# Spectral filter with gated FFN: scratch laid out by sides, filters copied inside SBUF, the sine table turned by DMA

## The chip, the cores and the metric

The kernel runs on one core of one Trainium2 chip. The metric is device time in microseconds (us) of one execution; the figure of a kernel is the median of its runs. The profiled execution is one more run, with its own time, and every duration below comes from its trace. The engines are named as in the profile: PE (TensorE matmuls), PEld (its weight loads), DVE (VectorE), ACT (ScalarE), POOL (GpSimd) and SP (SyncE, which here only issues DMAs).

## The reference, cut to what matters

x is 2048 rows (S) of 640 (D). Each row is normalized; the result goes through a two-dimensional real FFT, a pointwise complex filter w_r + i w_i (2048 x 321) and the inverse FFT, and beside it through a gated feed-forward network with 1536 inner columns (F). The two meet in the last line.

```
xn = (x - mean) / sqrt(var + 1e-5)
s  = irfft2(rfft2(xn) * (w_r + 1j * w_i))
g  = silu((gelu(xn @ w_gate) * (xn @ w_up)) @ w_down)
out = x + s * g
```

## The kernel before

**The two streams of work.** The FFN is the bulk: four groups of four slabs (a slab is 128 rows of x, taken with a stride of 16: row 16*n2 + n1 belongs to slab n1). For each group, `ffn_half` makes 12 tiles of gate and up products (psg and psu, L714), ACT takes the GELU of the gate (L718), DVE multiplies (L720), and `down_third` multiplies with w_down (L738). These pieces, in order, form the list `back`, 144 steps. The spectral branch is written as small pieces between them: `put(s, f, ...)` in lines 795 to 899 places a piece behind step s, and the loop at the end of `build` (L911) runs the steps. The whole order on each engine is thus written by hand (manual schedule); every engine and SP works through its own list in that order, and waits where its next instruction's inputs are not there.

**The spectral branch.** The FFT along the rows (length 2048 = 128 x 16) is done in two stages, with a product along the columns (length 640) between them.
- `tinv_sin` makes the sine table Tinv (128 x 16 x 128, bf16) on ACT, and `tfwd` turns it: for each of two halves, eight TensorE transposes into PSUM (L326) and one DVE copy into Tfwd (L327). They stand behind steps 26 and 27, between pieces of the first group's w_down product.
- `slab_S1` (from step 30 on) multiplies one folded slab with its part of Tfwd (pz, L484); ACT copies the result to zbuf (L486).
- `group_D` takes one slab first and then three at a time through the column transform FT (`d_group`, L494 and L498), copies to the buffer zd, and stores to the DRAM scratch ZDR, one store for each slab (L512). zd and zbuf lie in GEN, a buffer whose place B2 takes later.
- `load_B2` (behind step 56) reads ZDR back in another order, so that the second stage finds its 16 x 2 x 2 x 2 index combinations on the partitions: ten loads into 64 partitions each (L530). The stored order has re/im outermost, and the side (bit 5 of the row index) inside.
- `s2_in` and `s2_out` do the second stage and the filter in 11 bursts: products px (L556), an ACT copy xs (L564), two DVE multiplications with W1 and W2 (L568), products pu (L583), ACT copies, and stores to the scratch UDR (L592), 64 partitions each.
- `load_V` (behind step 89) reads UDR into one tile V in B2's place, in five pieces of 2, 2, 4, 4 and 4 slabs, re and im apart: ten loads (L603). `gather` (DVE, L613) picks the columns that don't fill a chunk; `slab_S1i` (L631), `group_Di` and the rest invert the transform and finish the rows.

**The filters.** W1 and W2 (128 x 2 x 16 x 322, bf16, 321 columns used) hold w_r and w_i so that the partition's two low bits are ri (re or im) and pm (row u or its mirror image 128 − u). `w_rows` loads them straight from DRAM, in rows of 321 elements (642 bytes) into 16 partitions of one half (hh); since both values of ri want the same data, each row is read twice. There are 18 loads for each filter: W1's behind steps 8 to 15, W2's behind 32 to 47. `w_edge` (POOL, L127) then halves the first and last column.

**Queues.** All DMAs are issued from SP, in one order; each also waits for the DMA issued eight places before it (eight semaphores are used in turn). The DMA transposes of slabs (`slab_T` with eng 2, L465: one 128 x 640 slab into xnT, five 128 x 128 blocks) stand in the same queue. xnT1, for the second FFN group, is made by the four of steps 17 to 23 and is first read at step 36.

Of the kernel before, what the change touches and what calls it, by code (L numbers as in the profile page):

```python
# [14 lines left out]
P = 128  # L15
S = 2048
D = 640
L = 321
# [12 lines left out]
@with_exitstack  # L31
def kernel(
    ctx: ExitStack,
    tc: tile.TileContext,
    A_x: bass.AP,
    A_w_r: bass.AP,
    A_w_i: bass.AP,
    B_x: bass.AP,
    B_w_gate: bass.AP,
    B_w_up: bass.AP,  # L40
    B_w_down: bass.AP,
    out: bass.AP,
):
# [26 lines left out]
    W2 = wts.tile([P, 2, NS, LP], BF16)  # L70
    wgv = B_w_gate.rearrange("(c p) f -> p c f", p=P)
    wuv = B_w_up.rearrange("(c p) f -> p c f", p=P)
    with tc.manual_schedule():
        build(nc, locals())


def build(nc, env):
# [33 lines left out]

    def w_rows(i, hh, ri, pm):
        WT, sp = spw[i]
        p0 = hh * 64 + ri * 2 + pm
        for lo in range(2):
            u0 = lo * 32 + hh * 16
            if pm == 0:
                nc.sync.dma_start(out=WT[p0:p0 + 61:4, lo, :, 0:L], in_=sp[:, u0:u0 + 16, :])
            elif u0 == 0:
                nc.sync.dma_start(out=WT[p0:p0 + 61:4, lo, 1:NS, 0:L], in_=sp[:, 127:112:-1, :])  # L120
                nc.sync.dma_start(out=WT[p0:p0 + 61:4, lo, 0, 0:L], in_=sp[:, 64, :])
            else:
                nc.sync.dma_start(out=WT[p0:p0 + 61:4, lo, :, 0:L], in_=sp[:, 128 - u0:112 - u0:-1, :])

# [108 lines left out]
    def affine(name, src, a, b):  # L233
# [84 lines left out]

    def tinv_sin():
        nc.scalar.activation(out=Tinv, in_=vt, func=ACT.Sin, bias=negpi, scale=TWO_PI / 2048.0)  # L320

    def tfwd(h):
        sl = slice(8 * h, 8 * h + 8)
        pt = psB.tile([P, 8, P], BF16, tag="b")
        for k in range(8):
            nc.tensor.transpose(out=pt[:, k, :], in_=Tinv[:, 8 * h + k, :], identity=ident)  # L326
        nc.vector.tensor_copy(out=Tfwd[:, sl, :], in_=pt)  # L327

# [129 lines left out]
    def slab_T(n1, eng):  # L458
# [17 lines left out]
    zbuf = fv.rearrange("p g l -> p (g l)").bitcast(BF16)[:, 0:4 * D].rearrange("p (s c k) -> p s c k", s=4, c=5)  # L476
    zdbuf = vt.rearrange("p n k -> p (n k)").bitcast(BF16)[:, 0:12 * LP].rearrange(
        "p (s a c l) -> p s a c l", s=2, a=3, c=2)

# [24 lines left out]
    def group_D(i):  # L504
        n0, n = DF[i]
        pd = d_group([Zt.pop(n0 + a) for a in range(n)], FT, LH)
        zd = zdbuf[:, i % 2, 0:n]
        for b in range(2):
            ev = nc.vector.tensor_copy if i in (2, 5) and b == 1 else nc.scalar.copy
            ev(out=zd.rearrange("p a c (m b) -> p a c m b", b=2)[:, :, :, :, b], in_=pd[b])  # L510
        for a in range(n):
            nc.sync.dma_start(out=ZDR[:, n0 + a].rearrange("c p l -> p c l"), in_=zd[:, a, :, 0:L])  # L512

# [10 lines left out]
    def load_B2():  # L524
        B2 = big.tile([P, NH, L], BF16, tag="sB", name="B2")
        zv = ZDR.rearrange("c n (z a k h) l -> a (c n z) k h l", z=2, a=2, k=2)
# [43 lines left out]

    uv = UDR.rearrange("c n (z a k h) l -> a (c n z) k h l", z=2, a=2, k=2)

    def s2_out(b):
# [16 lines left out]
        if l0 + w == L:  # L590
            for lo in range(2):
# [4 lines left out]
    VP = ((0, 2), (2, 2), (4, 4), (8, 4), (12, 4))  # L596
    VO = (0, L + 1, LH, L + 1 + HD)

    def load_V():
        V = big.tile([P, NS, 2 * L], BF16, tag="sB", name="Vin")  # L600
        for n0, n in VP:
            for c in range(2):
                nc.sync.dma_start(out=V[:, n0:n0 + n, c * L:c * L + L],  # L603
                                  in_=UDR[c].rearrange("n p l -> p n l")[:, n0:n0 + n, :])
        st_c["V"] = V
        st_c["Y"] = big.tile([P, NS, D], BF16, tag="sX", name="Yall")

    def gather(i):
        n0, n = VP[i]
        V = st_c["V"][:, n0:n0 + n, :]  # L610
        vr = work.tile([P, 4, P], BF16, tag="p1", bufs=2, name="vr")[:, 0:n, :]
# [14 lines left out]
    def slab_S1i(n1):  # L626
        V = st_c["V"]
        pv = psB.tile([P, 5, P], FP32, tag="b")
        for c in range(5):
            lhsT = V[:, n1, VO[c]:VO[c] + P] if c < 4 else st_c[("r", n1)]  # L630
            nc.tensor.matmul(pv[:, c, :], lhsT=lhsT, rhs=Tinv[:, n1, :], start=True, stop=True)  # L631
# [191 lines left out]
    put(23, fold_a, 0)  # L823
    for it in ((silu_table,), (tinv_sin,), (ft_sin, 0)):
        put(23, *it)
# [3 lines left out]
    put(25, fold_a, 1)  # L829
    put(26, tfwd, 0)  # L830
    put(27, tfwd, 1)
    put(27, norm, 8)
# [31 lines left out]
    for k in range(4):  # L864
        put(32 + 3 * k, slab_T, 8 + k, 2)
        put(65 + 3 * k, slab_T, 12 + k, 2)
    for k in range(16):
        put(8 + k if k < 8 else (32, 35, 38, 41, 44, 44, 47, 47)[k - 8], w_rows, k // 8, k % 8 // 4, k % 2, k % 4 // 2)
    put(40, w_edge, 0)
# [76 lines left out]
```

## Time and profile before

| | us |
|---|---|
| median of three runs (203.82 to 204.15) | 203.82 |
| the profiled execution | 204.42 |
| its span | 202.6 |
| PE busy | 195.6 |
| DVE busy | 129.3 |
| ACT busy | 122.4 |
| PE, L326 (the 16 transposes of Tinv) | 2 x 0.45 |
| DVE, L327 (two copies of 128 x 1024) | 2 x 0.69 |
| DVE, L568 (22 filter products, 646 ns each on average) | 13.3 |

The span is the time from the first instruction to the last; the execution's own time is larger by what lies around it (1.8 us). The page's busy figures are unions over the span, so an engine that is busy for 97% has almost no idle time to give back. In lists of groups, "x22 | 13.3, 646" means 22 instructions, 13.3 us in all, 646 ns on average, followed by the idle time of the engine before them and what ended it. In a timeline a line begins with the start and the duration in us. SPq lines are issues of DMAs: their duration is the time that SP needed to issue them, not that of the transfer; the time to landing is given in the DMA view.

### The profile page before, as it was taken

The numbers are of one execution on the slowest core, as the hardware profiler recorded it, in microseconds if no ns is written. First come the engines' busy times: TensorE is split into PE (matmuls) and PEld (weight loads), VectorE is DVE, ScalarE is ACT, GpSimd is POOL, SyncE is SP. The second block draws the span as 40 slices with busy tenths as digits, with TensorE's granted clock in tenths as the row PEclk, the third lists the DMA queues.
The fourth block names the chain that finished last, engine by engine and source line by source line (L and its number), as shares of the span: only waits on it lengthen the run. The fifth ranks groups of instructions, "written<-read, shape, count | busy, mean of one in ns | idle before, by whom it ended". The sixth has DMA issues, their size and how long they took to land.

```text
span 202.6 us, 4209 instructions
## 1 busy us (share of the span) xinstructions
PE 195.6 (97%) x1574; PEld 119.8 (59%) x1589; DVE 129.3 (64%) x340; ACT 122.4 (60%) x208; POOL 33.4 (16%) x61
## 2 busy tenths in 40 slices
PE   7899999999999999999999999999999999999993
PEld 5688854777555555566644333457775555556762
DVE  7886966786488982533576465342358776867672
ACT  2448657857886768423788688425375647476631
POOL 5327779953000200100000000000000000000000
PEclk9999999999999999999999999999999999999999
DMA  5999999899799999729995233569501334224211
GB/s 167 306 297 305 372 310 142 158 147 137 153 170 143 173 174 174 180 43 226 213 228 111 44 97 101 130 164 317 172 0 68 97 102 127 69 92 144 86 69 60
DMA packets 43315, 31.77 MB, mean 157 GB/s; under 512 B 12192, under 2 KB 41504, under 8 KB 43296
## 3 DMA queue, kind: packets, MB, share of 16 engines
q1 hardware_dynamic: 43296, 31.52, 71.4%
q8 instruction: 12, 0.20, 0.4%
q14 instruction: 7, 0.06, 0.1%
HBM read 21.66 MB, written 7.88 MB: 146 GB/s over the span
## 4 chain that ended last, share of the span: by engine, by line
PE 90%; DVE 4%; DMA 2%; issue 1%; POOL 1%; SPq 0%; ACT 0%; DVEq 0%
PE psu L714 25%; PE psg L714 24%; PE psg L738 13%; PE psu L738 12%; PE pd L494 5%; PE pz L484 2%; PE pv L631 2%; PE pu L583 2%; DMA X<-in_A_x_dram 2%; PE px L556 2%; PE pd L498 2%; DVE st L174 1%; DVE uT L720 1%; POOL rst L190 1%; PE pt L326 0%
## 5 line engine op out<-in xcount | busy, mean ns | idle before, releaser
L714 PE MATMUL psu<-xnT,Wu 128*128 128x512 bf16 (+2 forms) x289 | 60.9, 339 | 0.6 <-issue 0.2
L714 PE MATMUL psg<-xnT,Wg 128*128 128x512 bf16 (+2 forms) x286 | 60.4, 338 | 0.9 <-issue 0.5
L720 DVE TENSOR_TENSOR uT<-psu,ge 128x512 bf16<-128x512 f32 (+2 forms) x59 | 34.3, 585 | 29.8 <-PE psu L714 22.5
L718 ACT ACTIVATE ge<-psg 128x512 bf16<-128x512 f32 (+2 forms) x59 | 30.5, 518 | 27.6 <-PE psg L714 25.9
L738 PEld LDWEIGHTS <-uT 128*128 128x128 bf16 x384 | 36.3, 98 | 14.6 <-issue 0.6
L714 PEld LDWEIGHTS <-Wu 128*128 128x128 bf16 x295 | 26.6, 98 | 22.9 <-issue 2.7
L714 PEld LDWEIGHTS <-Wg 128*128 128x128 bf16 x295 | 26.6, 98 | 21.9 <-issue 1.5
L738 PE MATMUL psg<-Wd,uT 128*128 128x320 bf16 (+1 forms) x192 | 30.3, 302 | 0.0
L738 PE MATMUL psu<-Wd,uT 128*128 128x320 bf16 (+1 forms) x192 | 29.2, 296 | 0.0
L568 DVE TENSOR_TENSOR X<-xs,W 128x972 bf16<-128x972 bf16 (+2 forms) x22 | 13.3, 646 | 10.6 <-ACT xs L564 10.6
L174 DVE BATCH_NORM_STATS2 st<-X 128x6 f32<-128x320 bf16 x32 | 14.2, 482 | 0.5 <-DMA X<-in_A_x_dram 0.3
L633 ACT CAST W<-pv 128x640 bf16<-128x640 f32 x16 | 11.1, 692 | 5.4 <-PE pv L631 5.4
L510 ACT CAST GEN<-pd 128x966 bf16<-128x966 f32 (+1 forms) x10 | 10.4, 1102 | 5.3 <-PE pd L498 5.3
L656 ACT ACTIVATE W<-pd 128x960 bf16<-128x960 f32 (+2 forms) x14 | 10.1, 780 | 5.0 <-PE pd L498 5.0
L486 ACT CAST GEN<-pz 128x640 bf16<-128x640 f32 x16 | 11.0, 697 | 3.2 <-PE pz L484 3.2
L589 ACT CAST X<-pu 128x486 bf16<-128x486 f32 (+4 forms) x22 | 12.3, 558 | 0.3
L564 ACT CAST xs<-px 128x972 bf16<-128x972 f32 (+2 forms) x11 | 10.3, 936 | 2.4 <-PE px L556 2.4
L190 POOL TENSOR_TENSOR rst<-ve,mhalf 128x1 f32<-128x1 f32 (+2 forms) x9 | 6.5, 717 | 29.5 <-DVE ve L188 29.5
L662 DVE TENSOR_TENSOR W<-W 128x960 bf16<-128x960 bf16 (+1 forms) x12 | 6.8, 599 | 4.8 <-ACT W L656 4.8
L689 DVE TENSOR_TENSOR Yall<-Yall,G 128x640 bf16<-128x640 bf16 (+3 forms) x18 | 8.1, 450 | 2.1 <-ACT G L743 1.9
L747 DVE SCALAR_TENSOR_TENSOR G<-th,psu 128x320 bf16<-128x320 f32 x8 | 3.9, 488 | 8.4 <-ACT th L746 8.4
L452 DVE TENSOR_TENSOR f<-uvt 128x512 bf16<-128x512 bf16 x16 | 6.7, 421 | 3.0 <-PE pz L484 2.9
(137 smaller groups left out, 202.5 us busy)
## 6 DMA issues: line engine op xcount, KB each, us to landing
ZDR<-GEN SPq DMA_DIRECT2D x16, 160.5 KB, 5.3
xt<-in_A_x_dram SPq DMA_DIRECT2D x8, 320.0 KB, 3.5
UDR<-X SPq DMA_DIRECT2D x10, 240.8 KB, 3.6
W<-in_A_w_r_dram SPq DMA_DIRECT2D x14, 160.5 KB, 7.7
W<-in_A_w_i_dram SPq DMA_DIRECT2D x14, 160.5 KB, 6.0
out_dram<-Yall SPq DMA_DIRECT2D x14, 160.0 KB, 1.8
B<-ZDR SPq DMA_DIRECT2D x8, 240.8 KB, 5.5
Vin<-UDR SPq DMA_DIRECT2D x6, 321.0 KB, 6.3
```

The costliest lines, as they stand in the source:

```text
L174: nc.vector.bn_stats(out=st[:, k, :], in_=X[:, n1, 320 * k:320 * k + 320])
L486: nc.scalar.copy(out=Zt[n1], in_=pz)
L494: nc.tensor.matmul(out[a][g], lhsT=lhs[a][:, g, :], rhs=T[:, g, 0:w], start=(a == 0), stop=False)
L510: ev(out=zd.rearrange("p a c (m b) -> p a c m b", b=2)[:, :, :, :, b], in_=pd[b])
L564: nc.scalar.copy(out=xs, in_=px[:, :, 0:n * w].rearrange("p k (h l) -> p k h l", l=w))
L568: nc.vector.tensor_tensor(out=pp[-1], in0=xs, in1=WT[:, :, h0:h0 + n, l0:l0 + w], op=ALU.mult)
L589: nc.scalar.copy(out=us[:, :, :, c0:c0 + (w + 1 - m) // 2], in_=pv[:, :, :, m:w:2])
L633: nc.scalar.copy(out=vs, in_=pv)
L714: nc.tensor.matmul(ps, lhsT=WT[:, c, t * P:(t + 1) * P], rhs=xnT[g][:, c, c0:c1_], start=(c == 0), stop=(c == 4))
L718: nc.scalar.activation(out=ges[t], in_=ps, func=ACT.Gelu_apprx_tanh)
L720: nc.vector.tensor_tensor(out=uT[g][:, t, c0:c1_], in0=ps, in1=ges[t], op=ALU.mult)
L738: nc.tensor.matmul(ph, lhsT=uT[g][:, t, j * P:(j + 1) * P], rhs=Wd[:, t, c0:c1_], start=(t == 0), stop=(t == NT - 1))
```

## The change

Four things change at once.
- **Scratch by sides.** ZDR and UDR get the side as outermost index. `group_D` stores a group with four DMAs (side by re/im), each of 64 partitions taken with a step of 2; `load_B2` and `s2_out` then move all 128 partitions with one DMA for each hh, where they moved 64 for each side. To match, the bits of the partition index behind the tables are put in another order (`kh_f`, `u_f`).
- **Filters copied in SBUF.** Only the partitions of re are loaded from DRAM: `w_plus` in runs of 16 rows (10,272 bytes, which is why the tiles are now 321 wide), `w_minus` in rows as before; `w_twin` copies them to the partitions of im by a DMA from SBUF to SBUF, 32 partitions of 20,544 bytes.
- **Separate tiles.** zd becomes a tile of its own with two buffers. V's first four slabs stay in B2's place, the other twelve go to W2's, with four loads for each part.
- **The turned table.** `tinv_sin` runs in two halves, and `tfwd` becomes four DMA transposes issued from SP (four blocks of 128 x 128 each), behind steps 24 to 27; PE's transposes and DVE's copies are gone.

On SP the new order around the table is: W1's nine loads, the four xnT1 transposes, the four Tfwd transposes, W1's first twin, the first two ZDR stores, W1's second twin.

```
-    ZDR = dram.tile([2, NS, P, L], BF16)
-    UDR = dram.tile([2, NS, P, L], BF16)
+    ZDR = dram.tile([2, 2, NS, 64, L], BF16)
+    UDR = dram.tile([2, 2, NS, 64, L], BF16)
...
-    W1 = wts.tile([P, 2, NS, LP], BF16)
-    W2 = wts.tile([P, 2, NS, LP], BF16)
+    W1 = wts.tile([P, 2, NS, L], BF16)
+    W2 = wts.tile([P, 2, NS, L], BF16)
...
-    def w_rows(i, hh, ri, pm):
...
+    def w_plus(i, hh, lo):
+        WT, sp = spw[i]
+        p0 = hh * 64
+        u0 = lo * 32 + hh * 16
+        nc.sync.dma_start(out=WT[p0:p0 + 61:4, lo].rearrange("p h l -> p (h l)"),
+                          in_=sp[:, u0:u0 + NS, :].rearrange("k h l -> k (h l)"))
+
+    def w_minus(i, hh, lo):
+        WT, sp = spw[i]
+        p0 = hh * 64 + 1
+        u0 = lo * 32 + hh * 16
+        if u0 == 0:
+            nc.sync.dma_start(out=WT[p0:p0 + 61:4, lo, 1:NS, :], in_=sp[:, 127:112:-1, :])
+            nc.sync.dma_start(out=WT[p0:p0 + 61:4, lo, 0, :], in_=sp[:, 64, :])
+        else:
+            nc.sync.dma_start(out=WT[p0:p0 + 61:4, lo, :, :], in_=sp[:, 128 - u0:112 - u0:-1, :])
+
+    def w_twin(i, pm):
+        v = spw[i][0].rearrange("p a h l -> p (a h l)")
+        nc.sync.dma_start(out=v[2 + pm:P:4], in_=v[pm:P:4])
...
-    u_f, hi_f, s_f, h_f, pf, n1_f, z_f = bits(
-        "pb", [(0, 63), (6, 1), (0, 31), (5, 1), (0, 127), (1, 15), (0, 1)])
+    kh_f, hi_f, s_f, h_f, pf, n1_f, z_f = bits(
+        "pb", [(1, 31), (6, 1), (0, 31), (5, 1), (0, 127), (1, 15), (0, 1)])
...
-    u64 = fma("u64", e64, 64.0, u_f)
+    u64 = fma("u64", e64, 64.0, fma("u_f", z_f, 32.0, kh_f))
...
-    def tinv_sin():
-        nc.scalar.activation(out=Tinv, in_=vt, func=ACT.Sin, bias=negpi, scale=TWO_PI / 2048.0)
-
-    def tfwd(h):
         sl = slice(8 * h, 8 * h + 8)
-        pt = psB.tile([P, 8, P], BF16, tag="b")
-        for k in range(8):
-            nc.tensor.transpose(out=pt[:, k, :], in_=Tinv[:, 8 * h + k, :], identity=ident)
-        nc.vector.tensor_copy(out=Tfwd[:, sl, :], in_=pt)
+        nc.scalar.activation(out=Tinv[:, sl, :], in_=vt[:, sl, :], func=ACT.Sin, bias=negpi, scale=TWO_PI / 2048.0)
+
+    def tfwd(q):
+        sl = slice(4 * q, 4 * q + 4)
+        nc.sync.dma_start_transpose(out=Tfwd[:, sl, :], in_=Tinv[:, sl, :].rearrange("p n k -> p (n k)"))
...
-        zd = zdbuf[:, i % 2, 0:n]
+        zd = work.tile([P, 3, 2, LP], BF16, tag="zd", bufs=2, name="zd")[:, 0:n]
...
-        for a in range(n):
-            nc.sync.dma_start(out=ZDR[:, n0 + a].rearrange("c p l -> p c l"), in_=zd[:, a, :, 0:L])
+        for a in range(2):
+            if n == 1:
+                nc.sync.dma_start(out=ZDR[a, :, n0].rearrange("c p l -> p c l"), in_=zd[a:P:2, 0, :, 0:L])
+            else:
+                for c in range(2):
+                    nc.sync.dma_start(out=ZDR[a, c, n0:n0 + n].rearrange("n p l -> p n l"),
+                                      in_=zd[a:P:2, :, c, 0:L])
...
-            for lo in range(2):
-                nc.sync.dma_start(out=B4[64 * lo:64 * lo + 64, :, h0:h1, :], in_=zv[lo][:, :, h0:h1, :])
+            for hh in range(2):
+                nc.sync.dma_start(out=B4[:, hh, h0:h1, :], in_=zv[:, hh, h0:h1, :])
...
-            for lo in range(2):
-                nc.sync.dma_start(out=uv[lo][:, :, h0:h0 + n, :], in_=us[64 * lo:64 * lo + 64, :, :, :])
+            for hh in range(2):
+                nc.sync.dma_start(out=uv[:, hh, h0:h0 + n, :], in_=us[:, hh, :, :])
...
-        V = big.tile([P, NS, 2 * L], BF16, tag="sB", name="Vin")
-        for n0, n in VP:
+        Va = big.tile([P, VA, 2 * L], BF16, tag="sB", name="Vin")
+        Vb = W2.rearrange("p a h l -> p (a h l)")[:, 0:(NS - VA) * 2 * L].rearrange("p (n l) -> p n l", l=2 * L)
+        for V, n0, n1 in ((Va, 0, VA), (Vb, VA, NS)):
             for c in range(2):
...
-    for it in ((silu_table,), (tinv_sin,), (ft_sin, 0)):
+    for it in ((silu_table,), (tinv_sin, 0), (tinv_sin, 1), (ft_sin, 0)):
...
-    put(26, tfwd, 0)
-    put(27, tfwd, 1)
+    for q in range(4):
+        put(24 + q, tfwd, q)
...
+    WL = [(hh, lo) for lo in range(2) for hh in range(2)]
+    for i, places in enumerate(((8, 9, 10, 11, 12, 13, 14, 15, 30, 31), (32, 32, 35, 35, 38, 38, 41, 41, 47, 48))):
+        for k in range(4):
+            put(places[2 * k], w_minus, i, *WL[k])
+            put(places[2 * k + 1], w_plus, i, *WL[k ^ 1])
+        for pm in range(2):
+            put(places[8 + pm], w_twin, i, pm)
```

More of the change, by code (lines that the diff above doesn't have):

```diff
@@ L525, in load_B2 @@
         B2 = big.tile([P, NH, L], BF16, tag="sB", name="B2")
-        zv = ZDR.rearrange("c n (z a k h) l -> a (c n z) k h l", z=2, a=2, k=2)
+        zv = ZDR.rearrange("a c n (z k h) l -> (a c n z) k h l", z=2, k=2)
         B4 = B2.rearrange("p (k h) l -> p k h l", k=2)
         for h0, h1 in ((0, 3), (3, 6), (6, 9), (9, 12), (12, 16)):
-            for lo in range(2):
-                nc.sync.dma_start(out=B4[64 * lo:64 * lo + 64, :, h0:h1, :], in_=zv[lo][:, :, h0:h1, :])
+            for hh in range(2):
+                nc.sync.dma_start(out=B4[:, hh, h0:h1, :], in_=zv[:, hh, h0:h1, :])
         st_b["B2"] = B2
@@ L569, in s2_in @@
         st_b[b] = pp
-    uv = UDR.rearrange("c n (z a k h) l -> a (c n z) k h l", z=2, a=2, k=2)
+    uv = UDR.rearrange("a c n (z k h) l -> (a c n z) k h l", z=2, k=2)
     def s2_out(b):
@@ L590, in s2_out @@
         if l0 + w == L:
-            for lo in range(2):
-                nc.sync.dma_start(out=uv[lo][:, :, h0:h0 + n, :], in_=us[64 * lo:64 * lo + 64, :, :, :])
+            for hh in range(2):
+                nc.sync.dma_start(out=uv[:, hh, h0:h0 + n, :], in_=us[:, hh, :, :])
     st_c = {}
     VP = ((0, 2), (2, 2), (4, 4), (8, 4), (12, 4))
+    VA = 4
     VO = (0, L + 1, LH, L + 1 + HD)
     def load_V():
-        V = big.tile([P, NS, 2 * L], BF16, tag="sB", name="Vin")
-        for n0, n in VP:
+        Va = big.tile([P, VA, 2 * L], BF16, tag="sB", name="Vin")
+        Vb = W2.rearrange("p a h l -> p (a h l)")[:, 0:(NS - VA) * 2 * L].rearrange("p (n l) -> p n l", l=2 * L)
+        for V, n0, n1 in ((Va, 0, VA), (Vb, VA, NS)):
             for c in range(2):
-                nc.sync.dma_start(out=V[:, n0:n0 + n, c * L:c * L + L],
-                                  in_=UDR[c].rearrange("n p l -> p n l")[:, n0:n0 + n, :])
-        st_c["V"] = V
+                for a in range(2):
+                    nc.sync.dma_start(out=V[a:P:2, :, c * L:c * L + L],
+                                      in_=UDR[a, c, n0:n1].rearrange("n p l -> p n l"))
+        st_c["V"] = [Va[:, n, :] if n < VA else Vb[:, n - VA, :] for n in range(NS)]
+        st_c["Vp"] = [Va[:, n0:n0 + n, :] if n0 < VA else Vb[:, n0 - VA:n0 - VA + n, :] for n0, n in VP]
         st_c["Y"] = big.tile([P, NS, D], BF16, tag="sX", name="Yall")
@@ L609, in gather @@
         n0, n = VP[i]
-        V = st_c["V"][:, n0:n0 + n, :]
+        V = st_c["Vp"][i]
         vr = work.tile([P, 4, P], BF16, tag="p1", bufs=2, name="vr")[:, 0:n, :]
@@ L626, in slab_S1i @@
     def slab_S1i(n1):
-        V = st_c["V"]
+        V = st_c["V"][n1]
         pv = psB.tile([P, 5, P], FP32, tag="b")
         for c in range(5):
-            lhsT = V[:, n1, VO[c]:VO[c] + P] if c < 4 else st_c[("r", n1)]
+            lhsT = V[:, VO[c]:VO[c] + P] if c < 4 else st_c[("r", n1)]
             nc.tensor.matmul(pv[:, c, :], lhsT=lhsT, rhs=Tinv[:, n1, :], start=True, stop=True)
@@ L866, in build @@
         put(65 + 3 * k, slab_T, 12 + k, 2)
-    for k in range(16):
-        put(8 + k if k < 8 else (32, 35, 38, 41, 44, 44, 47, 47)[k - 8], w_rows, k // 8, k % 8 // 4, k % 2, k % 4 // 2)
+    WL = [(hh, lo) for lo in range(2) for hh in range(2)]
[5 more added lines that the diff above has]
+            put(places[8 + pm], w_twin, i, pm)
     put(40, w_edge, 0)
```

12 lines of the change are left out of this document (1 added, 11 removed).

## The prediction

> **What bounds the kernel now.** I read the page's busy shares and its chain first. TensorE (PE) is busy for 97% of the span at an undisturbed clock, and the chain that ended last is almost all PE.
>
> ```profile
> PE 195.6 (97%) x1574; PEld 119.8 (59%) x1589; DVE 129.3 (64%) x340; ACT 122.4 (60%) x208; POOL 33.4 (16%) x61
> PEclk9999999999999999999999999999999999999999
> PE 90%; DVE 4%; DMA 2%; issue 1%; POOL 1%; SPq 0%; ACT 0%; DVEq 0%
> ```
>
> So between the head (15 us) and the tail (4.6 us) only two things move the time: PE work removed, and PE made to wait. Next, the chain in order of time shows the PE work that the change takes away:
>
> ```profile
> 38.48 0.45 PE pt L326 x8
> 40.02 0.45 PE pt L326 x8
> ```
>
> Then the timelines of PE and of SyncE (SP), from which every DMA of this kernel is issued in order:
>
> ```profile
> 43.56 0.44 PE L484 MATMUL pz<-Tfwd,f 128*128 128x128 bf16 x5
> ```
>
> ```profile
> 18.82 2.76 SPq L84 DMA_DIRECT2D X<-in_A_x_dram  x1
> 33.24 0.53 SPq L121 DMA_DIRECT2D W<-in_A_w_r_dram  x1
> 38.98 2.74 SPq L123 DMA_DIRECT2D W<-in_A_w_r_dram  x4
> 41.89 7.95 SPq L465 DMA_TRANSPOSE xnT<-X  x4
> 49.94 0.53 SPq L512 DMA_DIRECT2D ZDR<-GEN  x1
> ```
>
> The first product that reads Tfwd runs at 43.56 (its weight load starts at 43.42). SP at that moment is two xnT transposes deep, behind the W1 loads, with two more to issue. The new Tfwd transposes stand behind those four. This queue is the heart of the case. The DMA view adds the time to landing of single issues (one stretch each):
>
> ```profile
> X<-in_A_x_dram SPq DMA_DIRECT2D x1, 640.0 KB, 13.3
> W<-in_A_w_r_dram SPq DMA_DIRECT2D x1, 160.5 KB, 7.8
> xnT<-X SPq DMA_TRANSPOSE x1, 2.8
> ```
>
> They are the X load issued at 18.82 (landed 32.1), the last W1 load, issued at 41.11 (48.9), and the fourth transpose, issued at 48.60 (51.4). The first of the four, issued at 41.89, took 7.6 us and landed at 49.5: the transposes moved only when the W1 loads ahead were through.
>
> Last, the PE timeline where B2 is first read, and a burst later:
>
> ```profile
> 93.52 0.83 PE L556 MATMUL px<-B,MG 64*64 64x162 bf16 x5
> 96.55 0.40 PE L556 MATMUL px<-B,MG 64*64 64x159 bf16 x5
> ```
>
> The same five products take 0.83 and 0.40 us: the first set waits inside for the second B2 load (issued 89.69, landing 4.2 later, 93.9). PE loses about 0.4 us there.
>
> **The change part by part.** The profiled execution took 204.42 us (span 202.6, 1.8 around it); the median of the runs is 203.82. I sum differences and set them on both.
>
> *Transposes off TensorE.* 16 products, 2 x 0.45 = 0.90 us of PE, all on the path: −0.90. Two DVE copies (692 ns each) go too, and with them 1.0 us of DVE waits; DVE is not the bound, so 0.
>
> *Tfwd by DMA.* Four transposes of four 128x128 blocks join SP's queue behind the xnT ones, which stand behind the W1 loads. PE waits for the first quarter alone (four of the 16 slabs); the next is wanted some 10 us later. PE would be at that weight load at 43.42 − 0.90 = 42.5. When does the quarter land?
> - Before, from the X load at 32.1 to the last W1 load at 48.9 there are 16 loads of 160 KB and two of 10 KB: about 1.05 us each. After, four loads in 642-byte rows stay, with one of 10 KB, and four become rows of 10,272 bytes: 4.5 us and 4 times an unknown. Bounds for the unknown: 1.05 (no gain from long rows) and 0.4 (160 KB at the 390 GB/s of the page's X and weight loads). Nearest row: the B2 loads, also long rows into one half of the partitions, 240.8 KB every 1.2 us, so 0.8 for 160.5 KB. I take 0.85. W1 is through at 40.0 (38.2 to 40.8). With the twins moved behind, that is nine us sooner than before.
> - The fourth xnT transpose landed 2.5 us after the last W1 load: 42.5 (40.7 to 43.3). One more of four blocks, at 2.5/4 x 4/5 = 0.5, lands at 43.0 (41.2 to 43.8).
> - SP's own limit: the first xnT transpose can be issued at about 33.9 (after the 10 KB load has landed); four at 1.23 us end at 38.8, and 2.8 to landing gives 41.6, so the queue of data decides. If issuing blocks as before (four in 7.95 us), the quarter is issued at 41.9 and lands at 44.4.
> PE's wait: 0.5, from 0 to 1.9. The slowest DMA ring sets these times, and its last loads run alone and faster; I take 0.4.
>
> The Trainium skill ("VectorE: DVE Perf Modes", The three transpose paths) gives 1309 ns for a 128x128 transpose by DMA against 390 by TensorE, and prefers TensorE where PSUM will do. By that price the quarter takes 5.2 us, lands at 47.7, and the sum would be about +4.1 us (a dearer form of the first rival below). The trace disagrees: four transposes of five blocks land within 2.5 us of the last W1 load, 0.13 us a block, so this price gets no chance of its own.
>
> *Sine in two halves.* ACT pays one more instruction's fixed cost, 0.2 us at most (a 1-element activation takes 0.20). ACT's next reader on PE, the FT product at 44.93, is over 5 us behind FT (written by 38.95): 0.
>
> *W2 and the twins.* W1's twins (2 x 657 KB inside SBUF) wait on SP for W1, and the stores of ZDR stand behind them. POOL's edge step waits for the twins; the next thing on POOL, a root at step 41, is over 5 us later, and W1 is first read at 95.4. W2 was complete at 83.5. Covered by 10 us or more: 0.
>
> *Odd rows.* With W rows of 321 every second row starts 2 bytes off a 4-byte boundary. L568 does 22 products on them, 660 ns each. I price this at 0: the gather L613 already reads rows at column 289 beside rows at even columns, and all six of that form take 222 ns; and L568 itself has rows of 159 elements (660 ns for 954), so its pairs straddle words already.
>
> *ZDR and B2.* Four stores of 123 KB per group replace three of 160 KB; the three before B2 land about 1.1 us apart, so bytes decide, and one more issue costs up to 0.5. Each B2 load then fills 128 partitions, not 64: 240.8 KB at 1.2 us becomes at best 0.65 (rate of the weight loads). The second lands at 93.9 + 0.4 − 0.9 = 93.4, when PE arrives at 93.5. Its wait of 0.4 goes: −0.35. If the rate stays, the wait grows to 0.8: +0.4.
>
> *V in two tiles.* PE's first V product (137.75) and DVE's first gather (136.45) now need all of the first four loads, not two. They are the same 657 KB; the fourth landed at 133.55 + 4.6 = 138.15 before. If that recurs, the gather ends at 138.4 and PE waits 0.7 to 0.9; if it lands like the third (136.2), nothing. I take 0.1. The other twelve slabs are wanted at 145.6 by a gather; V and xt together had landed by 146.5, and xt (640 KB) now comes after V, so V is in by 144.5: 0.
>
> *Constants.* One more 0.15 us operation on DVE before the first statistics; DVE idles 0.28 us before X's second slab: 0.
>
> Sum: −0.90 + 0.4 − 0.35 + 0.1 = −0.75, which is 203.67 for the profiled execution and 203.07 on the median.
>
> **Rivals.**
>
> *Tfwd comes late (slower).* One mechanism: SP issues the xnT transposes as slowly as before, or long rows bring nothing, and the first quarter lands at 44.4. PE waits 1.9: −0.90 + 1.9 − 0.35 = +0.65, 204.5. It decides from a landing after 43.8 on. For it: the 7.95 us of SP for four transposes. Against: the full rings behind that are shorter now, as the long rows are few packets and half the loads are gone. 18 in 100.
>
> *The gain is eaten (no change).* A quarter landing 0.9 to 1.6 late, or V's fourth load late again (+0.8), or B2's second load not sooner: 203.4 to 204.2. 20 in 100.
>
> *Odd rows halve VectorE.* The doubled rate of two 16-bit inputs is 0.53 ns an element here ((421 − 218)/384 from L452 and L453); from PSUM in f32 it is 1.06 (L720). At that rate each product of L568 takes 0.51 us more, each burst 1.0. In the burst at 123.26 DVE ends at 124.49 and PE starts on its result at 124.84: 0.35 of slack, so 0.65 lost in ten bursts: about 209.6. The gather's rows speak against it: 5 in 100. The Trainium skill ("VectorE: DVE Perf Modes", Mode 2×_1P) asks for 4-byte alignment, which would make this happen; its page "Vector Engine (DVE) Microarchitecture Reference" (the checked rule on the modes) says alignment makes no difference, and the rows above agree with the second.
>
> **How the numbers follow.** About 0.2% (0.4 us) can be told from no change here. The forecast, with Tfwd at most 0.7 late and B2's wait gone, holds 0.50 (202.5 to 203.4), mostly faster; the eaten gain 0.20; late Tfwd 0.18; the odd rows 0.05; 0.07 for a wait I don't see, mostly on the slow side. So faster 0.52, same 0.20, slower 0.28. The range runs from the best case, no Tfwd wait and no B2 wait (−1.3, less 0.1), to late Tfwd without B2's gain (−0.90 + 1.9 + 0.1 = +1.1): 202.4 to 205.0; beyond it lie the odd rows and a few in 100 of the rest.
>
> **What would show it.** PE without L326 and L484's first set near 42.5 to 43 with at most 0.7 us of idle time before it; W1's last loads landing near 40; xnT landing by 43; the first px set at 0.4 us; L568 still at 660 ns. I am wrong if PE stands over 1 us before L484, if L568 takes over 1 us, or if PE stands before the first V product.

## The result and the profile after

The changed kernel takes 203.18 us (median of 6 runs, 203.04 to 203.38) against 203.82 (6 runs beside it): a ratio of 0.9958, 95% interval 0.9938 to 0.9978 (the two medians alone give 0.9969, which lies inside it). It is faster, by 0.64 us where 0.75 were predicted. The profiled execution took 203.13 us, with a span of 201.1.

The page's busy shares, its chain and the group that the odd rows could have slowed, after the change:

```profile
PE 194.5 (97%) x1558; PEld 118.9 (59%) x1573; DVE 128.1 (64%) x339; ACT 122.6 (61%) x209; POOL 34.0 (17%) x61
PE 91%; DVE 5%; issue 1%; POOL 1%; ACT 0%
L577 DVE TENSOR_TENSOR X<-xs,W 128x972 bf16<-128x972 bf16 (+2 forms) x22 | 13.3, 648 | 10.2 <-ACT xs L573 10.2
```

TensorE (PE) still bounds the kernel, with 1.1 us less of work. The filter products (L568 before, L577 now) take 648 ns on average against 646: odd rows cost nothing.

SP's timeline after the change (start, time to issue; these are issues, not transfers):

```profile
31.37 0.59 SPq L127 DMA_DIRECT2D W<-in_A_w_r_dram  x1
32.03 0.57 SPq L116 DMA_DIRECT2D W<-in_A_w_r_dram  x1
32.72 5.28 SPq L471 DMA_TRANSPOSE xnT<-X  x4
38.09 5.16 SPq L333 DMA_TRANSPOSE Tfwd<-Tinv  x4
43.30 0.59 SPq L131 DMA_DIRECT2D W<-W  x1
```

and, from the DMA view, the time to landing of three single issues in it, in this order: the last W1 load, the fourth xnT transpose, and Tfwd's first quarter:

```profile
W<-in_A_w_r_dram SPq DMA_DIRECT2D x1, 160.5 KB, 4.1
```

```profile
xnT<-X SPq DMA_TRANSPOSE x1, 2.6
```

```profile
Tfwd<-Tinv SPq DMA_TRANSPOSE x1, 2.5
```

W1 was through at 32.03 + 4.1 = 36.2, xnT1 at 36.77 + 2.6 = 39.4 and the quarter at 38.09 + 2.5 = 40.6. The four xnT transposes, which SP needed 7.95 us to issue before, took 5.28.

PE's timeline where Tfwd, B2 and V are first read:

```profile
42.58 0.44 PE L488 MATMUL pz<-Tfwd,f 128*128 128x128 bf16 x5
...
92.53 0.42 PE L565 MATMUL px<-B,MG 64*64 64x162 bf16 x5
95.17 0.40 PE L565 MATMUL px<-B,MG 64*64 64x159 bf16 x5
...
136.36 0.39 PE L644 MATMUL pv<-Tinv,Vin 128*128 128x128 bf16 x4
```

No line has idle time before it. The quarter was there 2 us before PE wanted it, and the first px set takes 0.42 us where it took 0.83. In these two executions PE's end moved from 199.17 to 197.79. That is 1.38 us, twice what the medians differ by, so something in the profiled execution of before was not typical. The first experiment, the kernel before once more, shows what.

### The profile page after: what moved, and what is told of

It reads as the page before. It is cut to its first block, busy times and chain, and to the rows that moved or that the text cites. A ratio compares the mean times of both kernels' runs of the same rounds, so it can differ in the third digit from the quotient of the medians.

```text
span 201.1 us, 4180 instructions
## 1 busy us (share of the span) xinstructions
PE 194.5 (97%) x1558; PEld 118.9 (59%) x1573; DVE 128.1 (64%) x339; ACT 122.6 (61%) x209; POOL 34.0 (17%) x61
## 3 DMA queue, kind: packets, MB, share of 16 engines
q1 hardware_dynamic: 39424, 32.04, 55.9%
## 4 chain that ended last, share of the span: by engine, by line
PE 91%; DVE 5%; issue 1%; POOL 1%; ACT 0%
PE psu L727 25%; PE psg L727 25%; PE psg L751 13%; PE psu L751 12%; PE pd L498 5%; PE pz L488 2%; PE pv L644 2%; PE pu L592 2%; PE pd L502 2%; PE px L565 2%; DVE st L182 1%; POOL rst L198 1%; DVE X L204 1%; DVE mva L187 0%; DVE uT L733 0%
## 5 line engine op out<-in xcount | busy, mean ns | idle before, releaser
L733 DVE TENSOR_TENSOR uT<-psu,ge 128x512 bf16<-128x512 f32 (+2 forms) x59 | 34.3, 584 | 30.1 <-PE psu L727 22.5
L751 PE MATMUL psu<-Wd,uT 128*128 128x320 bf16 (+1 forms) x192 | 29.2, 296 | 0.0
L577 DVE TENSOR_TENSOR X<-xs,W 128x972 bf16<-128x972 bf16 (+2 forms) x22 | 13.3, 648 | 10.2 <-ACT xs L573 10.2
L514 ACT CAST zd<-pd 128x966 bf16<-128x966 f32 (+1 forms) x10 | 10.4, 1100 | 5.3 <-PE pd L502 5.3
L703 DVE TENSOR_TENSOR Yall<-Yall,xt 128x640 bf16<-128x640 bf16 (+3 forms) x18 | 8.2, 455 | 0.6
## 6 DMA issues: line engine op xcount, KB each, us to landing
UDR<-X SPq DMA_DIRECT2D x10, 240.8 KB, 2.5
B<-ZDR SPq DMA_DIRECT2D x8, 240.8 KB, 4.2
```

Source lines behind the costliest of these rows:

```text
L577: nc.vector.tensor_tensor(out=pp[-1], in0=xs, in1=WT[:, :, h0:h0 + n, l0:l0 + w], op=ALU.mult)
L733: nc.vector.tensor_tensor(out=uT[g][:, t, c0:c1_], in0=ps, in1=ges[t], op=ALU.mult)
L751: nc.tensor.matmul(ph, lhsT=uT[g][:, t, j * P:(j + 1) * P], rhs=Wd[:, t, c0:c1_], start=(t == 0), stop=(t == NT - 1))
```

## The experiments

The theory going in: PE bounds the kernel, and the change gains what leaves PE. The turned table costs PE nothing because W1's loads no longer stand long in the queue ahead of it. The sides take the wait out of the first px set, and all else is hidden. The rivals: the filter loads are not what covers the table (a lighter queue after them is), or the sides bring nothing and the whole gain is the 0.9 of the transposes.

### The kernel before, again

> The kernel before, once more, as a control: the profiles showed PE's last product 1.38 us earlier after the change, while the medians differ by 0.64 only. If the profiled execution of before was a slow one, its span here is about 201.9 to 202.2 and the first px set loses less than 0.4 us; if it was typical, the span is 202.6 again, the px set takes 0.8 us, and the difference lies outside the span. Time 203.8 either way.

203.82 us (11 runs, 203.62 to 204.05), 0.9992 of the kernel before (0.9983 to 1.0): nothing moved. Its profiled execution, at 203.87, is nearer to the median than the first one (204.42), and differs from it in two places. The second slab of X landed at 5.68, where it landed at 5.99 in the first, and all of PE's work stands 0.3 earlier. And the first px set waits less. PE's timeline of this run:

```profile
43.24 0.44 PE L484 MATMUL pz<-Tfwd,f 128*128 128x128 bf16 x5
...
93.20 0.60 PE L556 MATMUL px<-B,MG 64*64 64x162 bf16 x5
96.01 0.40 PE L556 MATMUL px<-B,MG 64*64 64x159 bf16 x5
```

From one px set to the next is 2.81 here, 3.03 in the first profile and 2.61 where nothing waits (below). So the wait that the prediction priced at 0.4 was 0.42 in one execution of the same kernel and 0.20 in another. Against this profile the change moves PE's end by 198.64 − 197.79 = 0.85, which fits the medians better.

### The changed kernel with the table turned by TensorE

```
-    def tfwd(q):
-        sl = slice(4 * q, 4 * q + 4)
-        nc.sync.dma_start_transpose(out=Tfwd[:, sl, :], in_=Tinv[:, sl, :].rearrange("p n k -> p (n k)"))
+    def tfwd(h):
+        sl = slice(8 * h, 8 * h + 8)
+        pt = psB.tile([P, 8, P], BF16, tag="b")
+        for k in range(8):
+            nc.tensor.transpose(out=pt[:, k, :], in_=Tinv[:, 8 * h + k, :], identity=ident)
+        nc.vector.tensor_copy(out=Tfwd[:, sl, :], in_=pt)
```

> The changed kernel with the table turned by TensorE again (steps 26 and 27, with the DVE copies and the single sine). If the gain is the 16 products (0.90) and the B2 wait (0.4), this loses 0.9 us against the changed kernel: about 204.1 by the profile, and the first px set stays at 0.4 us. If the gain came from the lighter DMA queues as a whole, it keeps it: 203.2 to 203.4.

204.41 us (12 runs), 1.0026 of the kernel before (1.0014 to 1.0037). The turning alone is worth 1.1 to 1.2 us in the changed kernel (1.23 between the medians; 1.14 when each is set against the runs of the kernel before beside it, +0.50 and −0.64). The rest of the change, without it, makes the kernel slower. PE's timeline:

```profile
43.42 0.44 PE L490 MATMUL pz<-Tfwd,f 128*128 128x128 bf16 x5
...
93.39 0.78 PE L567 MATMUL px<-B,MG 64*64 64x162 bf16 x5
96.37 0.40 PE L567 MATMUL px<-B,MG 64*64 64x159 bf16 x5
```

The px wait is there, 0.37, in spite of the sides: the last store of ZDR, issued at 85.60, landed only at 89.90 (4.3 later; 3.1 in the changed kernel), and B2's loads behind it came as late. And pz stands at 43.42, 0.18 behind the 43.24 of the kernel before, though up to there it does the same work on PE. That part of the loss is old: it is there before the FFN's first products. DVE's timeline at the very start, first of the kernel before (second profile):

```profile
2.13 0.15 DVE L246 SCALAR_TENSOR_TENSOR u<-e,pb 128x1 f32<-128x1 f32 x1
2.20 0.15 DVE L235 TENSOR_SCALAR cq<-pb 128x1 f32<-128x1 f32 x1
...
2.88 0.16 DVE L246 SCALAR_TENSOR_TENSOR b_r<-hs,cq 128x1 f32<-128x1 f32 x1
2.99 0.06 DVE L220 MEMSET GEN<- 128x1 int32 x1
3.02 0.49 DVE L174 BATCH_NORM_STATS2 st<-X 128x6 f32<-128x320 bf16 x1
```

then of the changed kernel:

```profile
2.14 0.15 DVE L254 SCALAR_TENSOR_TENSOR u_f<-pb 128x1 f32<-128x1 f32 x1
2.32 0.16 DVE L254 SCALAR_TENSOR_TENSOR u<-e,u_f 128x1 f32<-128x1 f32 x1
2.40 0.15 DVE L243 TENSOR_SCALAR cq<-pb 128x1 f32<-128x1 f32 x1
...
3.07 0.16 DVE L254 SCALAR_TENSOR_TENSOR b_r<-hs,cq 128x1 f32<-128x1 f32 x1
3.16 0.49 DVE L182 BATCH_NORM_STATS2 st<-X 128x6 f32<-128x320 bf16 x1
```

The one added operation (u_f) feeds the next, which starts 0.18 behind it and 0.19 later than it did, where independent ones follow each other in 0.07. The statistics of the first slab start at 3.16 in all ten profiles with the new constants, whether that slab had landed at 3.00 or 3.13. In the four with the old ones they start 0.02 behind the landing, at 3.02 to 3.10. By the first product with Tfwd this has grown to 0.2; the next experiment shows it from the other side.

### The changed kernel without the sides

```
-            for hh in range(2):
-                nc.sync.dma_start(out=B4[:, hh, h0:h1, :], in_=zv[:, hh, h0:h1, :])
+            for lo in range(2):
+                nc.sync.dma_start(out=B4[64 * lo:64 * lo + 64, :, h0:h1, :], in_=zv[lo][:, :, h0:h1, :])
...
-    u64 = fma("u64", e64, 64.0, fma("u_f", z_f, 32.0, kh_f))
+    u64 = fma("u64", e64, 64.0, u_f)
```

(with ZDR and UDR, their stores and the loads of V to match, so the constants are those of before too)

> The changed kernel with ZDR and UDR laid out as before, three stores a group, and loads of B2 into 64 partitions. If the B2 wait went because each load fills 128 partitions, it comes back: the second B2 load lands 1.1 to 1.2 us behind the first, PE loses 0.3 to 0.5 us at the first px set, and the time is about 203.6. If it went because the queue before the stores is lighter, px stays at 0.4 us and the time at 203.2.

203.70 us (11 runs), 0.9989 (0.998 to 0.9997): 0.4 to 0.5 us above the changed kernel (−0.21 against the runs of the kernel before beside it, where the change has −0.64). PE's timeline:

```profile
42.31 0.44 PE L488 MATMUL pz<-Tfwd,f 128*128 128x128 bf16 x5
...
92.27 0.40 PE L560 MATMUL px<-B,MG 64*64 64x162 bf16 x3
93.00 0.39 PE L560 MATMUL px<-B,MG 64*64 64x486 bf16 x2 [0.33 <-DMA B<-ZDR]
95.60 0.40 PE L560 MATMUL px<-B,MG 64*64 64x159 bf16 x5
```

Both effects are here. With the old constants, pz comes at 42.31, 0.27 ahead of the changed kernel. With the old layout the px sets are 3.33 apart, a loss of 0.72. PE arrives 0.9 sooner than in the second profile of before, but the second B2 load lands only 0.4 sooner (92.95 for 93.37), so half of what the transposes freed is given back 50 us later. Without the sides, the rest of the change brings 0.2 us.

The DMA view shows what the layout does to the loads. From the first issue to the last landing, the ten B2 loads take 14.5 to 14.8 us in the four profiles with the old layout and 10.5 to 11.5 in the nine with the new one that have the same ten loads. The second load, which the first px set needs, gains less surely: it lands 1.1 to 1.2 us behind the first with the old layout, and 0.6 to 2.4 behind it with the new.

### The kernel before with the turning alone

```
-    def tinv_sin():
-        nc.scalar.activation(out=Tinv, in_=vt, func=ACT.Sin, bias=negpi, scale=TWO_PI / 2048.0)
...
+    def tfwd(q):
+        sl = slice(4 * q, 4 * q + 4)
+        nc.sync.dma_start_transpose(out=Tfwd[:, sl, :], in_=Tinv[:, sl, :].rearrange("p n k -> p (n k)"))
```

> The kernel before with the turned table alone: four DMA transposes behind the xnT ones, all 18 W1 loads still ahead of them. If the transposes can only move when the W1 loads are through (48.9 us in the trace of before, the fourth xnT at 51.4), the first quarter lands at about 52 to 52.5 and PE stands some 9.5 us before the first product on Tfwd: about 212.5. If DMA transposes pass the loads in the rings, PE waits little and the time is 203 to 204.

215.67 us (6 runs, 214.28 to 219.04), 1.0577 (1.0539 to 1.0615). PE's timeline, and the granted clock (the seventh figure of a row, ahead of the DMA share) in three stretches of the same run:

```profile
51.58 0.69 PE L482 MATMUL pz<-Tfwd,f 128*128 128x128 bf16 x5 [8.99 <-DMA Tfwd<-Tinv]
...
104.11 0.40 PE L554 MATMUL px<-B,MG 64*64 64x162 bf16 x3 [0.90 <-DMA B<-ZDR]
105.25 0.39 PE L554 MATMUL px<-B,MG 64*64 64x486 bf16 x2 [0.74 <-DMA B<-ZDR]
```

```profile
38.00:44.00 6.00, 4.58 (x34) 3.07 (x32) 3.43 (x13) 3.46 (x8) 4.62 (x13) 1.00 1.12 152
51.60:55.00 3.40, 3.40 (x21) 2.17 (x21) 0.00 (x0) 1.13 (x2) 0.00 (x0) 0.50 0.89 113
55.00:60.00 5.00, 5.00 (x49) 3.79 (x46) 3.05 (x11) 3.54 (x7) 0.95 (x2) 1.00 0.40 90
```

The stop came as expected. What was not expected is the clock: it fell to half in the middle of the stop (at 44.8, where PE's last product had ended at 42.6), and PE came back at half and ran so until 55.0 (the same products take 0.69 where they took 0.44), and again from 106.2 to 109.7, after the px stops. Some 3.5 us of work at half the clock cost 1.7 us, each time.

### The changed kernel with the old filter loads

```
-    def w_plus(i, hh, lo):
...
+    def w_rows(i, hh, ri, pm):
...
-        for pm in range(2):
-            put(places[8 + pm], w_twin, i, pm)
```

> The changed kernel with the 18 loads of each filter as before (every row read twice, in 642-byte rows, no copies inside SBUF), all else as changed, the DMA turning included. Theory 1 (the cover of the turned table is the W1 work taken out of the queue): W1's last load lands at 48 to 49, the first quarter of Tfwd at 51 to 52, TensorE stands 8.5 to 9 us before its first product with Tfwd, and the time is as bad as in the kernel with the DMA turning alone (215.67), less what the sides give: 213 to 216. Theory 2 (that kernel was slow for its old scratch layout, whose stores and loads share the queue): the stop before the first product with Tfwd goes or shrinks to under 3 us: 203 to 207.

211.33 us (4 runs), 1.0389 (1.0345 to 1.0432). PE's timeline, and the clock as above:

```profile
48.35 0.69 PE L480 MATMUL pz<-Tfwd,f 128*128 128x128 bf16 x5 [5.55 <-DMA Tfwd<-Tinv]
```

```profile
48.40:52.50 4.10, 4.10 (x24) 2.54 (x25) 0.00 (x0) 1.63 (x4) 0.00 (x0) 0.50 0.73 93
52.60:60.00 7.40, 7.40 (x77) 5.29 (x75) 5.54 (x18) 4.69 (x9) 1.50 (x2) 1.00 0.35 91
```

The first theory holds in kind: without the new filter loads the table comes late, whatever the scratch layout. It misses in size, 5.55 and not 9, since W1 was through at 44.6 and not at 48 to 49. I had left the tiles 321 wide. With no padding, the eight loads of unmirrored rows are joined to 10,272-byte packets; in the trace 642-byte packets fill the whole stretch of the kernel before, and here half of the loads are long.

### The old filter loads, halves alternating

```
-        put(8 + k if k < 8 else (32, 35, 38, 41, 44, 44, 47, 47)[k - 8], w_rows, k // 8, k % 8 // 4, k % 2, k % 4 // 2)
+        put(8 + k if k < 8 else (32, 35, 38, 41, 44, 44, 47, 47)[k - 8], w_rows, k // 8, k % 2, k % 8 // 4, k % 4 // 2)
```

> The kernel of the first theory's test (18 loads of each filter as before, DMA turning), only that successive pairs of W1's and W2's loads go to alternating halves of the partitions, where before eight or nine in a row went to the same half. Theory 1 (bytes and packets set the time of a load): 1.05 us for each load as before, W1 through at 48 to 49, TensorE stands 8.5 to 9 us, 213 to 216. Theory 2 (the half of the partitions sets it, and two halves take loads side by side): 0.7 us or less for each, as in the changed kernel, W1 through at 43.5 to 44.5, Tfwd's first quarter at 46.5 to 47.5, TensorE stands 4 to 5 us: 207.5 to 210.5.

209.89 us (4 runs), 1.0298 (1.0271 to 1.0326); W1 through at 43.5. PE's timeline:

```profile
47.74 0.48 PE L480 MATMUL pz<-Tfwd,f 128*128 128x128 bf16 x3 [5.04 <-DMA Tfwd<-Tinv]
```

Against the kernel just above, W1 is through 1.1 us sooner for 16 loads: the order of the halves counts a little, 0.07 us a load, not the 0.35 of the second theory.

### The changed kernel, halves not alternating

```
-    WL = [(hh, lo) for lo in range(2) for hh in range(2)]
+    WL = [(hh, lo) for hh in range(2) for lo in range(2)]
...
-            put(places[2 * k + 1], w_plus, i, *WL[k ^ 1])
+            put(places[2 * k + 1], w_plus, i, *WL[k])
```

> The changed kernel with W1's and W2's loads in the order of the halves (first all four of one half, then all four of the other; as changed, row loads and long-run loads alternate between halves). Theory 1 (only bytes and packets count): nothing moves, W1's last load at 36 to 36.5, Tfwd's first quarter at 40.5, 203.0 to 203.3. Theory 2 (alternating halves made the loads fast): each load takes 0.85 to 1.05 again, W1 through at 38.5 to 40.5, Tfwd's first quarter at 42 to 43.3, TensorE stands 0 to 0.8: 203.1 to 204.

202.95 us (5 runs), 0.9966 (0.9953 to 0.9979); W1 through at 37.35, Tfwd's first quarter at 41.1, PE doesn't stand. X landed 0.5 later than in the changed kernel; counted from there, W1 is between the theories, again some 0.1 us a load, and the time is that of the changed kernel.

### The long runs cut into rows

```
-        nc.sync.dma_start(out=WT[p0:p0 + 61:4, lo].rearrange("p h l -> p (h l)"),
-                          in_=sp[:, u0:u0 + NS, :].rearrange("k h l -> k (h l)"))
+        nc.sync.dma_start(out=WT[p0:p0 + 61:4, lo, :, :], in_=sp[:, u0:u0 + NS, :])
```

> The changed kernel with its long-run loads cut into 642-byte rows (the same bytes into the same partitions, in the same order). Theory 1 (row loads cost 1.05 us each, the figure that the prediction used): four loads at 1.05 in place of some 0.5 each, W1 through at 38.2 to 40.5, Tfwd's first quarter at 42 to 43.5, TensorE stands 0 to 1.0: 203.1 to 204.3. Theory 2 (half as many loads is what counts, and a row load in this order takes 0.7): W1 through at 36.8 to 37.2, Tfwd's first quarter by 41.5, TensorE doesn't stand, 203.0 to 203.4.

202.91 us (4 runs), 0.9961 (0.9946 to 0.9976), W1 through at 36.6. This told nothing apart: in tiles without padding the rows are joined again, and the queue has as many packets as in the changed kernel (39424). It is a repeat of the changed kernel. The test needs the padding:

```
-    W1 = wts.tile([P, 2, NS, L], BF16)
+    W1 = wts.tile([P, 2, NS, LP], BF16)
...
+        nc.sync.dma_start(out=WT[p0:p0 + 61:4, lo, :, 0:L], in_=sp[:, u0:u0 + NS, :])
```

> The changed kernel with W1 and W2 322 columns wide again (one column of padding after each 321, set to zero once by POOL), and the long-run loads cut into 642-byte rows, which in 322 columns cannot be joined. Eight loads in rows for W1 in place of four in rows and four in long runs; all else as changed, the copies inside SBUF included. Theory 1 (a load in 642-byte rows into rows of 644 takes 1.1 us, as in the kernel before): W1's last load at 39.5 to 41, Tfwd's first quarter at 43 to 44.3, TensorE stands 0.5 to 1.8 before it, 203.6 to 204.8. Theory 2 (half as many loads is all that counts, a load in rows takes 0.7 where fewer stand in the queue): W1 through at 36.8 to 37.5, Tfwd's first quarter by 41.7, TensorE doesn't stand, 202.9 to 203.3.

203.04 us (5 runs), 0.9964 (0.9951 to 0.9977). SP's timeline and the landing of the quarter:

```profile
33.53 0.55 SPq L116 DMA_DIRECT2D W<-in_A_w_r_dram  x1
34.18 5.41 SPq L474 DMA_TRANSPOSE xnT<-X  x4
39.68 5.17 SPq L336 DMA_TRANSPOSE Tfwd<-Tinv  x4
```

```profile
Tfwd<-Tinv SPq DMA_TRANSPOSE x1, 2.5
```

The last W1 load landed at 38.5 and the quarter at 42.2, while PE wanted it at 42.5: no stop. Here X's load before W1 landed late, at 32.7, so the first theory's window for W1 (39.5 to 41) would have to be later still; eight loads in rows took 5.9 us from there, 0.73 each. The second theory stands in kind: half as many loads is what counts. The margin (0.3 us here, 2 in the changed kernel) is smaller for two reasons: X landed 1.3 later, and eight loads in rows take 1.0 longer than four in rows and four in long rows (5.9 for 4.8).

The kernels side by side (one profile each), W1's loads counted from the landing of X's last load, which is ahead of them in the queue (the small loads of 10 KB left out of the count):

| kernel | loads | us | each | first quarter landed | PE stood | median us |
|---|---|---|---|---|---|---|
| before | 16 rows | 16.8 | 1.05 | – | 0 | 203.82 |
| turning alone | 16 rows | 15.9 | 0.99 | 51.4 | 8.99 | 215.67 |
| old loads | 8 rows, 8 runs | 12.9 | 0.81 | 48.2 | 5.55 | 211.33 |
| old loads, alternating | 8 rows, 8 runs | 11.8 | 0.74 | 47.6 | 5.04 | 209.89 |
| padded rows | 8 rows | 5.9 | 0.73 | 42.2 | 0 | 203.04 |
| halves not alternating | 4 rows, 4 runs | 5.5 | 0.69 | 41.1 | 0 | 202.95 |
| changed | 4 rows, 4 runs | 4.8 | 0.60 | 40.6 | 0 | 203.18 |

### The changed kernel again, and two versions to beat it

> The changed kernel itself once more, as the yardstick for the two that follow: 203.0 to 203.3. If the wait inside the first set of px products belongs to single executions and not to the kernel, this profile may show that set at 0.4 to 0.8 us.

203.09 us (7 runs, 202.89 to 203.78), 0.9965 (0.9952 to 0.9978). The profiled execution was the slowest of the seven, 203.78. PE's timeline:

```profile
92.51 0.39 PE L565 MATMUL px<-B,MG 64*64 64x162 bf16 x2
93.15 0.40 PE L565 MATMUL px<-B,MG 64*64 64x486 bf16 x3 [0.25 <-DMA B<-ZDR]
95.76 0.40 PE L565 MATMUL px<-B,MG 64*64 64x159 bf16 x5
```

Up to 92.5 it agrees with the first profile to 0.03; then the second B2 load takes 4.8 us from issue to landing (3.9 there), and 0.64 is lost, which is the whole difference between the two executions (203.78 − 203.13 = 0.65). So the px wait belongs to single executions: in the ten profiles with the new layout it was 0.64, 0.37, 0.14, 0.03 and six times nothing; in the four with the old layout it was there each time (0.20, 0.42, 0.72, and two stops of 1.6 together).

The first of the two versions makes the four last transposes of tables by DMA too:

```
-        for k in range(2):
-            nc.tensor.transpose(out=pt[:, k, :], in_=MG[:, k].rearrange("p d q -> p (d q)"), identity=ident)
...
+        nc.sync.dma_start_transpose(out=N1, in_=MG.rearrange("p a d q -> p (a d q)"))
+        nc.sync.dma_start_transpose(out=N2, in_=MJ.rearrange("p a d q -> p (a d q)"))
...
-    put(z_end + 3, mg_turn)
+    put(42, mg_turn)
```

> The changed kernel with the last four TensorE transposes of tables (the filter stage's MG and MJ, 0.22 us of TensorE at 85.7) made by two DMA transposes behind step 42, where DVE's two copies go too. Theory 1 (TensorE bounds, and nothing new waits): 0.2 less than the changed kernel, 202.8 to 203.0. Theory 2 (what is freed ahead of the px products is given back there, since B2's second load then comes too late): the same as the changed kernel within 0.1, with the first px set at 0.55 to 0.65 us or a gap of 0.2 before its second half.

203.10 us (8 runs), 0.997 (0.9959 to 0.9981), beside 203.09. PE's work did end sooner, at 197.52 against 197.74 in the profiles without a px wait, and the px set takes 0.40, so nothing was given back there; but the span is 201.0, as theirs (201.1). The last store landed 0.2 sooner and the time behind it was 0.2 longer. Whether 0.2 was won can't be told from these runs.

The second adds smaller first loads of B2:

```
-        for h0, h1 in ((0, 3), (3, 6), (6, 9), (9, 12), (12, 16)):
+        for h0, h1, l0, l1 in ((0, 3, 0, WB), (0, 3, WB, L), (3, 6, 0, L), (6, 9, 0, L), (9, 12, 0, L), (12, 16, 0, L)):
```

> The same with B2's first pair of loads cut into the columns of the first burst (162) and the rest (159), four loads of 120 KB in place of two of 240 KB. Theory 1 (bytes set the landing): the second load lands 0.5 to 0.8 sooner, the first px set always takes 0.4 us, and the time is 0.2 to 0.4 below that of the changed kernel: 202.6 to 202.9. Theory 2 (the number of row pieces sets it, which stays the same at half the size): the second load lands as before, and the other half of the columns comes later: 202.9 to 203.4.

203.24 us (12 runs), 0.998 (0.997 to 0.999): no gain. In its profile the second load landed 2.85 after its issue (the second load of 240.8 KB took 3.9 in the changed kernel), and the px set took 0.40, but that execution (203.74) started late: the second slab of X landed at 6.28, 0.5 later than in the changed kernel. Neither version beats the changed kernel by more than can be told.

## Why the prediction was right, and where its steps were not

- **Transposes off TensorE, −0.90.** Right; with the px wait that it meets, putting them back costs 1.1 to 1.2.
- **Tfwd by DMA, +0.4.** The result was 0, and the step that failed is "so the queue of data decides". W1 was through at 36.2, not 40.0, and xnT1 at 39.4, not 42.5. The quarter came when SP had issued it: 38.09 and 2.5 to land, almost the 38.8 and 41.6 that the prediction had as SP's own limit. The mis-sized term is the price of 1.05 us for a load in rows: W1's loads took 4.8 us from the landing of X, where the prediction has 7.9 (the other 0.7 is X itself, which landed at 31.35 and not at 32.07).
- **Why a load cost less.** Going from 16 loads in rows to eight (before to padded rows) saved 16.8 − 5.9 = 10.9, or 1.4 for each load that went, more than the average of any kernel. Part of this can be read in the traces. They have sixteen landing signals for each load, which I take as one from each of the 16 DMA engines (the prediction's rings). Of the sixteen signals of X's last load, 13 had come by 29.2 in the kernel before and 14 by 30.1 with padded rows, the last at 32.1 and 32.7. So most rings were at W1 some 3 us before the landing from which its loads were counted, for 16 loads as for 8. Counted from the first of these signals, a load in rows took (48.9 − 28.4)/16 = 1.28 in the kernel before. For the padded rows this price gives 29.3 + 8 x 1.28 = 39.5, the average from the landing 32.7 + 8 x 1.05 = 41.1, and the measured end is 38.5. So the head start would account for 1.6 of the 2.6 us. The alternating halves, at 0.07 to 0.1 us a load, would account for 0.6 to 0.8. Neither share was tested by a run of its own on these loads, and the rest is open.
- **A block turned by DMA.** The four quarters landed 1.3 us apart, 0.33 us a block, the pace at which SP issued them (5.16 us for four), and each 2.4 to 2.5 us after its issue. By the Trainium skill ("VectorE: DVE Perf Modes", The three transpose paths: 1309 ns for a 128x128 block) a quarter would have taken an estimated 5.2 us, so the trace disagrees again.
- **ZDR and B2, −0.35.** The direction is right: undone, it costs 0.72 in the trace, and 0.4 to 0.5 in the median, where the old constants give 0.27 back. The step behind it holds only in part. The loads got faster together (10.9 us for ten where the second profile of before has 14.6), but the second landed 1.6 behind the first, not the 0.65 that was priced; what brought it forward in this profile was the first, which landed 2.8 us after its issue for 3.7. The size is that of one execution; against the second profile of before it is 0.2. It was priced from a single trace of a wait that varies from run to run.
- **Constants, 0.** Wrong: +0.2. "DVE idles 0.28 us before X's second slab" was true of that execution, in which the slab landed late (5.99), and it looked at the wrong slab: the added operation stands ahead of the first one's statistics, where DVE has no slack. This is the term that the prediction's hidden work did not cover, and it hid behind the bigger gains.
- **V, +0.1.** Nothing: Va's four loads landed by 135.4, and PE's first V product came without a stop at 136.36.
- **Odd rows, twins and W2, the sine in halves: 0.** All as predicted; 648 ns with rows of 321 and 646 with the padded ones. The alignment that the Trainium skill ("VectorE: DVE Perf Modes", Mode 2×_1P) asks for made no difference here.
- **The sum.** Against the second profile of before, PE's end moved by −0.90 + 0.24 (pz at 42.58 for 43.24, where the transposes alone would make it 42.34) − 0.17 (px), close to the 0.85 measured; 0.11 of that is lost behind PE's end (5.34 from there to the execution's time, for 5.23). The medians show 0.64 and 0.58. So −0.75 was met by misses that cancel: the Tfwd wait was taken 0.4 too high, the constants 0.2 too low, the px wait some 0.2 too high and V 0.1 too high. The 0.9 of the transposes was foreseen; that the sum of the other terms came within 0.1 to 0.2 of the medians is luck.
- **The rivals.** Tfwd late is what happens where the filter loads stay as they were (5.0 to 9.0 us). Those stops cost clock as well, which its price leaves out; a stop of the 1.9 us that it priced was not seen, so whether that one would is open. That most of the gain is eaten by B2 is what happens without the sides.

Open: why 0.06 to 0.14 us at the first statistics become 0.2 at pz. In the changed kernel DVE's third multiplication of the FFN starts at 9.82, after 0.40 of waiting for PE, where it ran at about 9.3 before. Not tried: the extra constant moved behind the first slab's normalization, which by the profiles should bring 0.2.

## What to carry to other kernels

A transfer put on a queue is late by what stands ahead of it, so price the queue by counting from the first load that moves, not by averages from the landing of the load ahead: here that would have come nearer (39.5 where 38.5 was measured, against 41.1), since a head start doesn't shrink with the number of loads. Time freed on the bounding engine reaches the end only if the next load that it meets is ready as much sooner; here the turned table was worth 1.1 to 1.2 us with the sides, and without them half of its gain was waited away. And an operation of 0.15 us is not free because its engine is 64% busy: look at what stands right behind it, in more than one execution.

## What the hardware showed that was not expected

- While PE stood for 5.0 to 9.0 us, the granted clock fell to 0.50, 2.2 to 4.6 us after PE's last product, and it stayed there for 3.4 to 10.2 us in the clock record, the latter part of it after work had come back. So the stop of 9.0 us cost 1.7 us more, and the one of 5.55 us 2.1 more. In the turning-alone run it fell once more, for 3.4 us, after two stops of 0.90 and 0.74 us within 2 us.
- The same bytes in rows of 321 elements go to a tile of 321 columns in joined packets of 10,272 bytes, and to one of 322 columns in packets of 642: 12.9 us (old loads) against 15.9 (turning alone) for the 16 loads, of which half can be joined.
- Loads that alternate between the halves of the partitions took 0.07 to 0.1 us less each, in two pairs of profiles.
